# Sums of shared parts in two GpSimd operations instead of three, and masks made one step later

## The chip, the cores and the metric

The kernel runs on one core of a Trainium2 chip. The core's engines work side by side, each through its own list of instructions in order: TensorE (PE in the profile, with its weight loads as PEld), VectorE (DVE), ScalarE (ACT), GpSimd (POOL) and SyncE (SP), which here issues nearly all the DMAs. Engines wait for each other by semaphores. The metric is device time in microseconds; the kernel before takes 681.6 us (median of four runs, 679.55 to 683.3).

## The reference

Two blocks follow each other. The first is a delta-rule recurrence over 768 steps for 4 batches and 8 heads of width 48. In each step, with k normalised to length one:

```python
y[t]  = q[t] @ state
v_old = k[t] @ state
state = state + beta[t] * outer(k[t], v[t] - v_old)
```

The second takes the 4 x 768 outputs as 3072 tokens of width 384 and applies two dense layers with a hard swish between:

```python
h = x @ w_in                       # 384 -> 2048
g = h * clip(h + 3, 0, 6) / 6
out = g @ w_out                    # 2048 -> 384
```

## The kernel before

**The recurrence in chunks.** Time is cut into 24 chunks of 32 steps. The 4 batches times 32 steps fill the 128 partitions. For each chunk t a generator `prep(t)` makes what does not depend on the state, in steps: (1) GpSimd normalises the keys (`kb`, L502) and, where `whole` is set, makes the masks of the chunk at once (`mask(t)`, two multiplications at L478: beta times a fixed mask, for the even and the odd heads, into the tile `mb`); (2) TensorE transposes the keys (L518), ScalarE copies them to `KQ` (L526); (3) the same for the queries; (4) TensorE forms all products of keys with keys and queries (`sc`, L539); (5) VectorE multiplies them by the masks (L550, into `L` and `LB`), and GpSimd scales the keys by beta (`bkb`, L490). L550 is the only reader of `mb`, and `mb` has one buffer from chunk 9 on, so the masks of t wait until L550 of t-1 has read its own.

`chain(t)` then carries the state through the chunk (products with the state `ks` L798, `R` on VectorE at L892 and L898, `pz` and `py` L819, the update `su` L927, the output `y` L811 and L854, its transposition `yt` L864), and `inverse(g)` solves small triangular systems for four chunks at a time, element by element on VectorE (L751 and L756, alternating).

**The dense layers in blocks.** Two chunks make a block of 256 tokens. From block 5 on, `up_by_eleven` does the first layer by a scheme of Strassen's kind: for each of 8 products j it forms 2 x 2 tiles of 128 x 128 outputs out of 11 matmuls instead of 12. `begin(j)` issues the first four, which are parts shared by several outputs. ScalarE copies them from PSUM into the four quarters of a tile `g` (`gt`, L1069), and GpSimd adds them up there by `plus_minus` (L1020). `end(j)` issues the other seven matmuls on top of the same PSUM tile, and VectorE adds the sums from `gt` to PSUM tiles 3, 1 and 2 (L1085, L1086). ScalarE copies tile 0 (L1092), which lets the PSUM tile go, and makes the clipped factor (L1096); VectorE multiplies (L1099). PSUM tiles of this pool (`ph`, `pt`, `pz`, `py`, `yt`, `po`) come from one ring of four. `down_by_seven` does the second layer likewise with 7 products instead of 8 (L1211), sums on VectorE (L1197), and the sums of its outputs on GpSimd, on VectorE in the last block (both L1221). `weight_sums` makes sums of weights on GpSimd (also L1020, on 128x256) before the first such block.

**What sets the order.** The order of instructions on every engine is fixed when the program is built. A list written out by hand (`ORDER`) covers the first part. A loop over chunks follows, which cuts each chunk into 15 units and issues in each unit at most one step of `prep`, of `chain`, of the inverse and of the dense layers. `take(now)` in a unit's plan is one step of the chunk's `prep`. `plus_minus`, the masks, `kb`, `bkb`, the squares of keys (L401) and the output's sums share GpSimd's list, so what is issued first there is in front. Masks of chunks before the ninth are placed by `ORDER` and not by `prep`.

Of the kernel before, what the change touches and what calls it, by code (L numbers as in the profile page):

```python
# [15 lines left out]
ALU = mybir.AluOpType  # L16
# [30 lines left out]
def kernel(  # L47
# [21 lines left out]
    nc = tc.nc  # L69
# [3 lines left out]
    P = B * C  # L73
# [23 lines left out]
    def rows(b):  # L97
        return slice(C * b, C * b + C)
# [4 lines left out]
    def group(t):  # L103
        return (0, t) if t < G0 else ((t - G0) // GS + 1, (t - G0) % GS)
# [34 lines left out]
    def needs(*what):  # L139
        assert past.issuperset(what), (what, set(what) - past)  # L140
# [3 lines left out]
    def ring(tag, n, key):  # L144

        alive = [x for x in rings.get(tag, ()) if ("read", x) not in past]
        needs(*(("read", x) for x in alive[: max(len(alive) + 1 - n, 0)]))
        rings[tag] = alive + [key]
# [56 lines left out]
    for j, value in enumerate((1.0, -1.0)):  # L205
        m = mask2[:, j, :]
        for b in range(B):
            nc.gpsimd.memset(mask2[rows(b), j, :], value)
            nc.gpsimd.affine_select(
                out=mask2[rows(b), j, :], in_=mask2[rows(b), j, :], pattern=[[1, C]],  # L210
# [78 lines left out]
    def pad(t):  # L289
        return [f"pad{t}"] if t < NBKB else []  # L290
# [176 lines left out]
    def mask(t):  # L467
        early = t < LS + LE
        if t > 1 or not early:
            needs(("L", t - (2 if early else 1)))  # L470
        if early and t % 2 == 0:
            mb = mb_spare.rearrange("p (e a j w) -> p e a j w", e=2, j=2, w=C)
        else:
            mb = work.tile([P, 2, NP, 2, C], FP32, name="mb", bufs=1)
        mbs[t] = mb
        needs("beta")
        for e in range(2):
            nc.gpsimd.tensor_tensor(  # L478
                out=mb[:, e],
                in0=beta_tok[:, t, e:H:2].unsqueeze(2).unsqueeze(3).to_broadcast([P, NP, 2, C]),  # L480
                in1=mask2[:].unsqueeze(1).to_broadcast([P, NP, 2, C]),
                op=ALU.mult,
            )
        yield
# [12 lines left out]
    def prep(t, whole=True):  # L497

        g, i = group(t)
        kb, qb = kbufs[t % NKB], qbufs[t % NQB]  # L500
        needs(*([("bkb", t - NKB)] if t >= NKB else []), *(pad(t) if t < NKB and t else []))
        nc.gpsimd.tensor_tensor(  # L502
            out=kb[:, :, 0:D], in0=kfs[g][:, i],
            in1=invs.pop(t).unsqueeze(2).to_broadcast([P, H, D]), op=ALU.mult,
        )
        past.add(("kb", t))
        if whole:
            drain(mask(t))
        yield

        for j, src in enumerate((kb, qb)):
            if j == 1:
                needs(("q", t))
                past.add(("qT", t))
            ring("pm", NPM, ("pt", t, j))
            pt = psM.tile([128, NP, P], FP32, name="pt", tag="pm")
            for p in range(NP):
                nc.tensor.transpose(  # L518
                    pt[:, p, :], src[:, 2 * p : 2 * p + 2].rearrange("p e w -> p (e w)"), ident[:]
                )  # L520
            yield 1
            if j == 0:
                ring("KQ", NKQ, ("KQ", t))
                KQ = work.tile([128, NP * B // 2, 4, C], FP32, name="KQ", bufs=NKQ)
            read(("pt", t, j))
            nc.scalar.activation(  # L526
                out=KQ[:, :, 0:4:3, :] if j == 0 else KQ[:, :, 1:3, :],
                in_=pt[:].rearrange("q p (x y c) -> q (p x) y c", y=2, c=C), func=ACTF.Copy,
            )
            yield  # L530
        ring("pc", NPC, ("sc", t))
        sc = psC.tile([P, 2, 512], FP32, name="sc", tag="pc")
        scv = sc[:, :, 0 : NP * 2 * C].rearrange("p e (a j w) -> p e a j w", a=NP, j=2)
        for p in range(NP):
            for b in range(B):
                for e in range(2):
                    r = slice(DP * e, DP * e + DP)
                    kq = KQ[r, p * B // 2 + b // 2]
                    nc.tensor.matmul(  # L539
                        scv[rows(b), e, p],  # L540
                        lhsT=kq[:, 3 if b % 2 else 0, :],
                        rhs=kq[:, 3:1:-1, :] if b % 2 else kq[:, 0:2, :],
                        start=True, stop=True,
                    )
        yield
        needs(*([("BZ", t - NLB)] if t >= NLB else []))
        LB = work.tile([P, H, C], FP32, name="LB", bufs=NLB)
        mb = mbs.pop(t)
        for j, out in enumerate((lowers(t), LB)):
            nc.vector.tensor_tensor(  # L550
                out=out.rearrange("p (e a) w -> p e a w", e=2), in0=scv[:, :, :, j, :],
                in1=mb[:, :, :, j, :], op=ALU.mult,
            )
        past.add(("L", t))
        KQs[t], LBs[t] = KQ, LB
        read(("sc", t), *([("KQ", 0)] if t == 0 else []))
        if whole:
            drain(scaled(t))
        yield
# [459 lines left out]
    def plus_minus(out, a, b, op):  # L1019
        nc.gpsimd.tensor_tensor(out=out, in0=a, in1=b, op=op)  # L1020
# [28 lines left out]
    def up_by_eleven(blk):  # L1049
        needs(("sums", blk))  # L1050
        B11, T3x, B21, B22, B31, B32 = x_tiles(blk)
        phs, ready = {}, {}

        def mm(ph, n, w, x, start=False, stop=False):
            nc.tensor.matmul(  # L1055
                ph[:, n], lhsT=w, rhs=x, start=start, stop=stop, skip_group_check=True
            )

        def begin(j):
            key = ("ph", blk, "by", j)  # L1060
            ring("pm", NPM, key)
            ph = phs[j] = psM.tile([128, 4, P], FP32, name="ph", tag="pm")
            mm(ph, 0, W11[:, j], B11, start=True)
            mm(ph, 1, S1[:, j], T1x)
            mm(ph, 2, W21[:, j], T3x)
            mm(ph, 3, S2[:, j], T2x)
            gs[blk, j] = mlp.tile([128, 2, TB], FP32, name="g", bufs=NFC // 2)
            gt = gs[blk, j][:].rearrange("p i (t c) -> p (i t) c", c=P)
            nc.scalar.activation(out=gt, in_=ph[:], func=ACTF.Copy)  # L1069
            plus_minus(gt[:, 1], gt[:, 1], gt[:, 2], ALU.add)  # L1070
            plus_minus(gt[:, 2], gt[:, 0], gt[:, 1], ALU.add)
            plus_minus(gt[:, 0], gt[:, 0], gt[:, 3], ALU.add)

        def end(j):
            ph = phs.pop(j)
            mm(ph, 0, W12[:, j], B21)
            mm(ph, 1, S4[:, j], B22)
            mm(ph, 2, W22[:, j], T4x)
            mm(ph, 0, W13[:, j], B31)
            mm(ph, 1, W13[:, j], B32)  # L1080
            mm(ph, 2, W23[:, j], B31)
            mm(ph, 3, W23[:, j], B32, stop=True)
            g = gs[blk, j][:].rearrange("p i c -> p (i c)")
            gt = gs[blk, j][:].rearrange("p i (t c) -> p (i t) c", c=P)
            nc.vector.tensor_tensor(out=gt[:, 3], in0=ph[:, 3], in1=gt[:, 2], op=ALU.add)  # L1085
            nc.vector.tensor_tensor(  # L1086
                out=gt[:, 1:3], in0=ph[:, 1:3],
                in1=gt[:, 0].unsqueeze(1).to_broadcast([128, 2, P]), op=ALU.add,
            )

            def first():
                nc.scalar.activation(out=gt[:, 0], in_=ph[:, 0], func=ACTF.Copy)  # L1092
                read(("ph", blk, "by", j))
                ro = mlp.tile([128, CB, DM], FP32, name="o", bufs=1)
                r = ro[:].rearrange("p c m -> p (c m)")[:, 0 : 2 * TB]
                nc.scalar.activation(out=r, in_=g, func=ACTF.Relu, bias=half, scale=1.0 / 6.0)  # L1096

                def rest():
                    nc.vector.scalar_tensor_tensor(  # L1099
                        out=g, in0=r, scalar=1.0, in1=g, op0=ALU.min, op1=ALU.mult  # L1100
                    )

                ready[j] = rest

            ready[j] = first
            if j == NPR - 1:
                past.add(("up", blk))

        def go(j):
            if j in ready:  # L1110
                ready.pop(j)()

        begin(0)
        yield
        begin(1)
        yield
        for j in range(NPR):
            end(j)
            go(j - 1)
            if j + 2 < NPR:  # L1120
                yield
                begin(j + 2)
                go(j)
                yield
            else:
                go(j)
                if j == NPR - 1:
                    go(j)
                yield
# [197 lines left out]
    def drain(gen):  # L1327
        for _ in gen:
            pass
# [197 lines left out]
```

## Time and profile before

| | before |
|---|---|
| median of four runs | 681.6 us (679.55 to 683.3) |
| the profiled execution, its own time | 680.79 us |
| its span in the profile | 679.1 us |
| mean granted TensorE clock | 0.985 |
| PE, PEld busy | 640.5 us (94%), 581.1 us (86%) |
| DVE, ACT, POOL busy | 499.4 us (74%), 271.9 us (40%), 221.0 us (33%) |
| sums of shared parts (L1020 on g), 168 times | 79.8 us, mean 477 ns |
| masks (L478 into mb), 38 times | 26.9 us, mean 728 ns |
| additions to PSUM (L1085, L1086), 56 times each | 16.0 us, mean 285 ns; 23.8 us, mean 425 ns |

The profile is of one execution. Busy times of an engine are unions of its instructions' durations, and times in the text are counted from the start of the span. A group of instructions is named by line, engine and what it writes and reads (out<-in). Behind it stand how often it ran, its busy time and the mean of one, and the time that the engine stood idle just before, with what ended most of it. A row of a wait reads: who waited, for whom, total, how often, longest. A row of a timeline reads: start, duration, engine, line, operation, shapes, how many were merged. The blocks that use `up_by_eleven` start at about 342, 393, 445, 496, 544, 591 and 637 us. Each is followed by its `down_by_seven`.

### The profile page before, as it was taken

To read this page: it belongs to the slowest core of one execution; us is meant where nothing else is said; L and a number is where in the kernel's file an instruction comes from. 1 tells how busy PE (TensorE), PEld (TensorE's weight loads), DVE (VectorE), ACT (ScalarE), POOL (GpSimd) and SP (SyncE) were. 2 spreads that over 40 slices of the span, in tenths; PEclk is the share of its full clock that TensorE was granted. 3 is DMA by queue.
4 is the path that set the end of the run, shared out by engine and by line. 5 is a ranking of instruction groups with operands and counts; after the bars stand their busy time and mean duration, and the time that the engine had idled before them with its cause. 6 is when DMAs were issued, how large, how long until landed. Compare 5 with 4: busy or idle time off the path is not lost.

```text
span 679.1 us, 26940 instructions
## 1 busy us (share of the span) xinstructions
PE 640.5 (94%) x11768; PEld 581.1 (86%) x11768; DVE 499.4 (74%) x1226; ACT 271.9 (40%) x532; POOL 221.0 (33%) x376
## 2 busy tenths in 40 slices
PE   2668989999999999999999999999999999999997
PEld 2557877776688988988999999999999999999997
DVE  5888876888546689747888957998747998557264
ACT  5995777422242232232244244244234143143250
POOL 6240232102421131236165255065043151442340
PEclk9978889999999999999999999999999999999999
DMA  7994335502041030032030030020020020010000
GB/s 195 252 204 128 91 76 147 85 2 47 15 84 26 3 70 4 2 71 37 3 69 6 2 73 2 3 61 3 2 49 3 2 48 2 14 26 3 26 1 23
DMA packets 88501, 33.29 MB, mean 49 GB/s; under 512 B 80160, under 2 KB 83232, under 8 KB 88384
## 3 DMA queue, kind: packets, MB, share of 16 engines
q1 hardware_dynamic: 88128, 31.29, 20.8%
q8 instruction: 92, 1.51, 0.9%
q10 hardware_dynamic: 256, 0.30, 0.2%
q14 instruction: 25, 0.20, 0.1%
HBM read 26.84 MB, written 4.72 MB: 46 GB/s over the span
## 4 chain that ended last, share of the span: by engine, by line
PE 81%; DVE 7%; DMA 3%; ACT 2%; issue 2%; SPq 2%; POOL 1%; DVEq 0%; ACTq 0%; POOLq 0%
PE po L1211 26%; PE ph L1055 16%; PE ph L983 14%; PE po L1146 6%; PE pz L819 3%; PE ks L798 3%; PE py L819 3%; PE su L927 3%; PE pt L518 2%; PE sc L539 2%; SPq L1135 1%; ACT spare L348 1%; PE yt L864 1%; DMA out_dram<-o 1%; DMA kf<-in_k_dram 1%
## 5 line engine op out<-in xcount | busy, mean ns | idle before, releaser
L1055 PE MATMUL ph<-xT,w_in 128*128 128x128 f32 x784 | 122.9, 278 | 0.7 <-ACT KQ L526 0.7
L983 PE MATMUL ph<-xT,w_in 128*128 128x256 f32 (+1 forms) x576 | 116.2, 353 | 2.0 <-DVE g L994 1.5
L1211 PE MATMUL po<-w_out,g 128*128 128x192 f32 x640 | 110.6, 326 | 0.0
L983 PEld LDWEIGHTS ph<-xT,w_in 128*128 128x128 f32 x576 | 95.0, 194 | 14.3 <-DVE g L994 2.3
L1055 PEld LDWEIGHTS ph<-xT,w_in 128*128 128x128 f32 x784 | 103.9, 192 | 2.1 <-ACT KQ L526 0.9
L1020 POOL TENSOR_TENSOR g<-g 128x128 f32<-128x128 f32 x168 | 79.8, 477 | 76.5 <-ACT g L1069 67.3
L1211 PEld LDWEIGHTS po<-w_out,g 128*128 128x128 f32 x640 | 104.1, 190 | 0.2
L1211 PE MATMUL po<-spare,g 128*128 128x192 f32 x480 | 86.7, 332 | 0.0
L1211 PEld LDWEIGHTS po<-spare,g 128*128 128x128 f32 x480 | 77.2, 190 | 1.8
L1221 POOL TENSOR_TENSOR o<-o,u 128x192 f32<-128x192 f32 x18 | 18.6, 1033 | 167.3 <-ACT o L1218 93.5
L991 ACT ACTIVATE g<-ph,halves 128x256 f32<-128x256 f32 (+1 forms) x96 | 41.1, 436 | 79.1 <-PE ph L983 79.1
L1197 DVE TENSOR_TENSOR g<-g 128x256 f32<-128x256 f32 x160 | 62.8, 442 | 3.5 <-PE po L1211 3.1
L1069 ACT ACTIVATE g<-ph 128x512 f32<-128x512 f32 x56 | 33.4, 596 | 79.6 <-PE ph L1055 76.1
L756 DVE TENSOR_TENSOR A<-A,pr 128x30 f32<-128x30 f32 (+9 forms) x150 | 59.3, 395 | 3.6
L751 DVE TENSOR_TENSOR pr<-A 128x30 f32<-128x30 f32 (+9 forms) x150 | 56.1, 374 | 3.4
L348 ACT ACTIVATE spare<-spare,places 128x768 uint16<-128x768 uint16 (+1 forms) x56 | 52.4, 940 | 2.2 <-DMA spare<-in_moe_w_in_dram 1.3
L994 DVE SCALAR_TENSOR_TENSOR g<-g,ph 128x256 f32<-128x256 f32 (+1 forms) x96 | 35.0, 370 | 24.3 <-ACT g L991 24.1
L1099 DVE SCALAR_TENSOR_TENSOR g<-o,g 128x512 f32<-128x512 f32 x56 | 42.1, 751 | 8.1 <-ACT o L1096 8.1
L1096 ACT ACTIVATE o<-g,halves 128x512 f32<-128x512 f32 x56 | 40.4, 722 | 15.6 <-DVE g L1099 8.6
L1146 PE MATMUL po<-w_out,g 128*128 128x384 f32 x128 | 45.6, 493 | 0.0
L1218 ACT ACTIVATE o<-po 128x192 f32<-128x192 f32 x40 | 13.2, 330 | 80.6 <-PE po L1211 76.3
L478 POOL TENSOR_TENSOR mb<-beta_tok,mask 128x256 f32<-128x256 f32 x38 | 26.9, 728 | 56.2 <-DVE LB L550 56.2
(141 smaller groups left out, 991.2 us busy)
## 6 DMA issues: line engine op xcount, KB each, us to landing
kf<-in_k_dram SPq DMA_DIRECT2D x96, 48.0 KB, 3.0
qb<-in_q_dram SPq DMA_DIRECT2D x96, 48.0 KB, 3.1
vf<-in_v_dram SPq DMA_DIRECT2D x96, 48.0 KB, 2.2
out_dram<-o SPq DMA_DIRECT2D x92, 48.0 KB, 1.6
spare<-in_moe_w_in_dram SPq DMA_DIRECT2D x4, 768.0 KB, 6.7
w_out<-in_moe_w_in_dram SPq DMA_DIRECT2D x4, 768.0 KB, 6.3
w_out<-in_moe_w_out_dram SPq DMA_DIRECT2D x4, 768.0 KB, 6.1
spare<-in_moe_w_out_dram SPq DMA_DIRECT2D x4, 768.0 KB, 4.6
```

The source lines that it names most:

```text
L348: nc.scalar.activation(out=z, in_=z if n else d.bitcast(I16)[:, :, :, 3], func=func, bias=places[:, n : n + 1], scale=scale,)
L751: nc.vector.tensor_tensor(out=pv, in0=A[:, j + 1 :, j].unsqueeze(2).to_broadcast([n, w, j]), in1=A[:, j, 0:j].unsqueeze(1).to_broadcast([n ...
L756: nc.vector.tensor_tensor(out=A[:, j + 1 :, 0:j], in0=A[:, j + 1 :, 0:j], in1=pv, op=ALU.subtract)
L819: nc.tensor.matmul(ps[rows(place(b)), D * h : D * h + D], lhsT=m(h)[rows(b)], rhs=z[rows(b), D * at(h) : D * at(h) + D], start=True, stop= ...
L983: nc.tensor.matmul(ph[:, cols], lhsT=w_in[:, s, f * 128 : (f + 1) * 128], rhs=xT[:, s, cols], start=(s == 0), stop=(s == NKT - 1),)
L991: nc.scalar.activation(out=g, in_=ph, func=ACTF.Relu, bias=half, scale=1.0 / 6.0)
L1020: nc.gpsimd.tensor_tensor(out=out, in0=a, in1=b, op=op)
L1055: nc.tensor.matmul(ph[:, n], lhsT=w, rhs=x, start=start, stop=stop, skip_group_check=True)
L1099: nc.vector.scalar_tensor_tensor(out=g, in0=r, scalar=1.0, in1=g, op0=ALU.min, op1=ALU.mult)
L1146: nc.tensor.matmul(pos[c][:], lhsT=gs[blk, f // 2][:, f % 2, c * P : (c + 1) * P], rhs=w_out[:, f, :], start=(f == 0), stop=(f == NFC - 1),)
L1197: nc.vector.tensor_tensor(out=A(f, *out), in0=A(f, *a), in1=A(f, *b), op=op)
L1211: nc.tensor.matmul(ps[n][:], lhsT=A(f - f % 2, *a)[:, f % 2], rhs=b[:, f], start=(f == 0), stop=(f == HF - 1),)
```

## The change

It has two parts. In `begin`, with p0 to p3 for the four copied quarters of `gt`, the three additions before leave p1+p2 in quarter 1, p0+p1+p2 in quarter 2 and p0+p3 in quarter 0. After, one addition over two quarters at once, taken in descending order, leaves p0+p3 in quarter 3 and p1+p2 in quarter 2, and a second one leaves p0+p1+p2 in quarter 0. `end` is changed to match: the addition over two tiles, which now takes quarter 3, comes first, and the single one, which takes quarter 0, second. In `prep`, the masks are made in the step in which the transposed keys are copied, and no longer in the step in which the keys are normalised.

```diff
@@ prep @@
         past.add(("kb", t))
-        if whole:
-            drain(mask(t))
         yield
...
                 in_=pt[:].rearrange("q p (x y c) -> q (p x) y c", y=2, c=C), func=ACTF.Copy,
             )
+            if whole and j == 0:
+                drain(mask(t))
             yield
@@ up_by_eleven, begin @@
             nc.scalar.activation(out=gt, in_=ph[:], func=ACTF.Copy)
-            plus_minus(gt[:, 1], gt[:, 1], gt[:, 2], ALU.add)
-            plus_minus(gt[:, 2], gt[:, 0], gt[:, 1], ALU.add)
-            plus_minus(gt[:, 0], gt[:, 0], gt[:, 3], ALU.add)
+            plus_minus(gt[:, 3:1:-1], gt[:, 0:2], gt[:, 3:1:-1], ALU.add)
+            plus_minus(gt[:, 0], gt[:, 0], gt[:, 2], ALU.add)
@@ up_by_eleven, end @@
-            nc.vector.tensor_tensor(out=gt[:, 3], in0=ph[:, 3], in1=gt[:, 2], op=ALU.add)
             nc.vector.tensor_tensor(
                 out=gt[:, 1:3], in0=ph[:, 1:3],
-                in1=gt[:, 0].unsqueeze(1).to_broadcast([128, 2, P]), op=ALU.add,
+                in1=gt[:, 3].unsqueeze(1).to_broadcast([128, 2, P]), op=ALU.add,
             )
+            nc.vector.tensor_tensor(out=gt[:, 3], in0=ph[:, 3], in1=gt[:, 0], op=ALU.add)
```

## The prediction

> **What bounds the kernel now.** I read first the page's busy shares, then the chain of work that ended last, then a table of the seven stages in which the edited code runs (stretches of the span, with the busy time of each engine), then who TensorE (PE) waited for after 336 us, and at last single rows of GpSimd (POOL) and VectorE (DVE).
>
> ```profile
> PE 640.5 (94%) x11768; PEld 581.1 (86%) x11768; DVE 499.4 (74%) x1226; ACT 271.9 (40%) x532; POOL 221.0 (33%) x376
> PE 81%; DVE 7%; DMA 3%; ACT 2%; issue 2%; SPq 2%; POOL 1%; DVEq 0%; ACTq 0%; POOLq 0%
> ```
>
> POOL is busy a third of the span, and 1% of the last chain is its. The stages with the edited sums (the first three columns are the stretch, its length and PE's busy time; then weight loads, DVE, ACT, POOL):
>
> ```profile
> 342.00:369.00 27.00, 26.18 (x509) 25.31 (x509) 23.38 (x54) 13.03 (x26) 16.39 (x31) 1.00 0.23 46
> 393.50:420.00 26.50, 26.50 (x513) 25.81 (x512) 16.73 (x36) 13.25 (x27) 15.67 (x31) 1.00 0.25 48
> 445.00:472.00 27.00, 25.98 (x504) 24.86 (x504) 24.29 (x56) 12.88 (x27) 16.51 (x30) 1.00 0.19 39
> 496.00:522.00 26.00, 24.85 (x440) 24.21 (x439) 15.22 (x36) 12.45 (x25) 10.94 (x25) 1.00 0.16 33
> 544.50:570.00 25.50, 24.67 (x438) 24.04 (x437) 22.99 (x59) 12.68 (x25) 11.74 (x24) 1.00 0.16 34
> 592.00:616.50 24.50, 24.50 (x437) 23.90 (x437) 12.94 (x32) 12.57 (x25) 10.87 (x24) 1.00 0.12 27
> 637.50:660.00 22.50, 22.50 (x194) 22.50 (x194) 10.97 (x25) 12.27 (x25) 11.54 (x25) 1.00 0.07 19
> ```
>
> PE fills three of the seven to the last hundredth. In the others it lacks 0.8, 1.0, 1.2 and 0.8 us. Who it waited for from 336 us to the end:
>
> ```profile
> PE pz L819 <- DVE R L898: 2.2, 3, 1.1
> PE ph L1055 <- ACT KQ L526: 0.7, 1, 0.7
> PE py L819 <- issue: 0.6, 1, 0.6
> PE pz L819 <- ACT o L1218: 0.4, 1, 0.4
> PE yt L864 <- DVE y L854: 0.4, 1, 0.4
> ```
>
> POOL is not among them. All five together are 4.3 us of 343; the rows that name DVE are 2.6. DVE is said to wait for the edited sums:
>
> ```profile
> DVE g L1085 <- POOL g L1020: 14.4, 6, 2.8
> ```
>
> These six waits belong to the first two products of the stages at 496, 592 and 637 us. In the last of these, L1085 starts at 640.93, 643.38, 645.81 and 648.27, 2.45 us apart, the pace of PE's eleven matmuls, and only the first two are put down to POOL. The first product's three sums ended at 640.5 (two sets of three from 638.99, 2.99 us long), 0.45 us before L1085 began. So DVE waited for PE's last matmul there too, and the name POOL misleads. Of the gaps of PE, the one at 506.5 us (in the stage at 496) goes back through R (L898), which stands on DVE behind the product g<-o,g (L1099), to the wait of ACT L1096 for the output's DMA: the sums have no part in it.
>
> **The change, part by part.**
>
> *Two sums for three.* L1020 runs 168 times on 128x128 tiles, 79.8 us busy, 477 ns mean, three per product, 56 products. The trace has no GpSimd operation over two tiles in descending order. Nearest by form are the sums of weights on the same line, 128x256 from two tiles, 727 ns (median of the four rows 725 to 728). Bounds: the mask rows of the same size take 617 (median); the slowest plain add, o<-o,u at L1221, has a mean of 1033 ns on 192 elements, scaled to 256 some 1380. I take 727 since it is the same operation and size. A product then costs 727 + 477 = 1204 against 3 x 477 = 1431: 0.23 us less, 56 x 0.23 = 12.7 us of POOL time (bounds 19 less and 24 more). On the path: nothing, as POOL is not what PE waits for. The cover is the product itself: eleven matmuls of 224 ns (the last 176 rows, 88 loads and 88 matmuls, took 19.71 us), 2.46 us a product, in which POOL now works 1.52 us for a product and would work about 1.25.
>
> *The two DVE additions change places.* L1085 takes 0.29 us, L1086 0.42, and both still come before the ACT copy L1092. Before, the first waited for two POOL sums by what it read, and the second for the third; by the new order the first writes both middle tiles, one of which the second POOL sum reads, so it waits for both POOL sums, and the second adds nothing to wait for. Sum 0.71 us as before. I cost it at nothing: DVE comes to L1085 at PE's pace, with the sums 0.45 us ready. If a sum were late after all, the next cover is the ring of four PSUM tiles; past that room, each 0.1 us by which DVE is late costs PE 0.1 us a product, 5.6 us over 56. The ring's room: in the last stage the first product's tile is let go by L1092 at 642.48 and wanted by the fifth product at 645.5 (637.2 + 4 products' beginnings of 0.9 and 3 ends of 1.57, PE never idle), 3.0 us later.
>
> *The masks one step later.* By the order of the two programs on each engine, only five of the masks pass anything on POOL. Apart from the swapped additions no other engine's order changes; DMA queues and SP hold the same issues in the same order. The three in the edited stages:
>
> ```profile
> 345.38 0.98 POOL L502 TENSOR_TENSOR kb<-kf,inv 128x384 f32<-128x384 f32 x1
> 346.33 1.34 POOL L478 TENSOR_TENSOR mb<-beta_tok,mask 128x256 f32<-128x256 f32 x2
> 347.63 3.36 POOL L1020 TENSOR_TENSOR g<-g 128x128 f32<-128x128 f32 x6
> 351.62 1.80 POOL L1020 TENSOR_TENSOR g<-g 128x128 f32<-128x128 f32 x3 [0.63 <-ACT g L1069]
> 355.95 0.42 DVE L550 TENSOR_TENSOR L<-sc,mb 128x256 f32<-128x256 f32 x1
> ```
>
> The six sums that stood behind the mask now stand ahead of it. The first set can start at 346.4; the second needs the ACT copy that ends at 348.2, so it ends near 349.5; the mask then runs to about 350.8, and L550, its only reader, asks at 355.95: 5.1 us of room. Behind the mask stand the sums that wait for ACT until 351.55 anyway. At 396 and 447 the same count gives ends at 401.9 (copy ended 399.55, sums to 400.7) and 453.0, against readers at 406.22 and 458.45: 4.3 and 5.4 us. Cost nothing; the cover is that room. The third set's copies there end at 402.88 and 454.44, later than the masks. The fourth move lets six sums of weights (727 ns) pass a mask that waits for LB until 304.55:
>
> ```profile
> 293.62 0.83 POOL L502 TENSOR_TENSOR kb<-kf,inv 128x384 f32<-128x384 f32 x1
> 304.69 1.19 POOL L478 TENSOR_TENSOR mb<-beta_tok,mask 128x256 f32<-128x256 f32 x2 [10.24 <-DVE LB L550]
> ```
>
> POOL sits idle there for 10.24 us; six sums fit into it, and the later sums end some 4 us sooner. Their reader is the stage at 342 and the last of them still waits for the addition at 328, so: nothing. The fifth move, near 175 us, puts one square (0.82) ahead of a mask that ends at 176.8 and is read at 184.66: nothing.
>
> *What is left is who disturbs whom on DVE.* The product L1099, a DVE operation with both inputs in SBUF, takes 0.68 us in most rows, and long ones lie where POOL is at work:
>
> ```profile
> 357.82 1.24 DVE L1099 SCALAR_TENSOR_TENSOR g<-o,g 128x512 f32<-128x512 f32 x1
> 368.15 1.22 DVE L1099 SCALAR_TENSOR_TENSOR g<-o,g 128x512 f32<-128x512 f32 x1
> ```
>
> Of its 56 rows, the 44 that hardly overlap POOL have a median of 682 ns; the 12 that do average 1001. So less POOL time is less DVE time where DVE has no idle. In the stage at 342, DVE works without a gap from 342.7 to R's second half (L898, 351.96), for which PE waits 0.25 us at 352.7. POOL drops about 3 x 0.23 = 0.7 us before it; DVE operations in it run at about 0.55 against 0.41 (the L751 and L756 rows on 234 to 240 elements), a third longer, so DVE gains 0.2 us, and so does PE. The same at 466.7, where PE waits 0.4 us for y (L854) behind a full DVE: 0.1 us. At 554 the wait goes back to the output's DMA as at 506: nothing. Sum: 0.3 us gained. Ends for this effect: a gain of the whole 2.6 us that PE waits for DVE. Against it, a longer POOL operation can hold a DVE operation longer: the 12 disturbed L1099 rows each by the added 727 - 477 = 0.25 us, 3.0 us lost if all of it lay ahead of PE.
>
> Here a page speaks against the change: the Trainium skill, "SBUF — State Buffer", section "Who interferes with whom", says that a DVE operation with two SBUF inputs and a GpSimd operation that reads SBUF shut each other out for a whole instruction, whichever began first. By it the longest hold grows with the POOL operation, and the sum would be 3 us slower instead of 0.3 us faster. The rows above (1.24 against 0.68) fit a hold of about one POOL operation, but do not tell how often one strikes.
>
> **Sum.** The profiled execution took 680.8 us (span 679.1 and 1.7 around it); less 0.3 gives 680.5. It lies 0.8 under the median of 681.6, so against the median I say 681.3. The four runs spread from 679.55 to 683.3, about 0.5%, which is what a measurement of this kernel can tell from no change (3.4 us).
>
> **The rivals.**
> *Faster:* all that PE waits for DVE goes. For: DVE is at 23.4, 24.3 and 23.0 us in the three crowded stages. Against: at 506 and 554 a DMA sets the wait. It gives 681.6 - 2.6 = 679.0. To pass 0.5% the two ACT rows, 1.1 us, would have to go too (677.9).
> *Slower, by holds on DVE:* one longer POOL operation a product holds the crowded DVE, R and y come late, PE waits at L819 and L864. It decides from the point where DVE loses more than the 2.5 to 3.6 us that it has idle in a crowded stage, or where a hold falls just ahead of L898. Price up to 3.0 us: 684.6.
> *Slower, by the descending order:* if the wide sum is no 727 ns but over 1.85 us, a product needs more than its 2.46 us on POOL, and lateness grows from product to product until the ring's 3 us are used up. At 3.0 us it would be 1.15 x 8 - 3 = 6 us a stage, 7 stages, over 720 us. Against: no add in the trace comes near that.
> *The change does nothing that counts:* POOL's time falls and all else stays: 681.6.
>
> **Chances.** Forecast with the case that nothing counts 0.78 (680.5 to 682, and the spread of the runs); faster rival 0.08, half of it past 0.5% by scatter; holds on DVE 0.11, a third past 0.5%; descending order 0.03. So faster 0.04, slower 0.07, same 0.89. The range takes both ends of the DVE effect: 679.0 to 684.4.
>
> **What would show it.** Right: L1020 with 56 wide rows near 0.73 us and 56 at 0.46 to 0.48, together near 67 us; L1085 still 2.45 us apart in the last stage, whomever its waits are put down to; no L550 row that waits for a mask; POOL's sums of weights from 294 us; PE's waits still these five. Wrong: a wide row over 1.4 us, L1099's mean above 751 ns, a PE wait for L898 or L854 longer than now, or a new PE wait ahead of L1055. It would be wrong altogether if a change to POOL's order moved PE somewhere before 336 us, where DVE and ACT set the pace.

## The result and the profile after

The changed kernel is slower: a median of 682.9 us against 680.6 for the kernel before on the same chips, a ratio of 1.0028 with a 95% interval of 1.0018 to 1.0037. The two medians lie 2.3 us apart; the ratio is some 1.9 us, and that is the figure used below. The forecast was 0.3 us faster.

The profiled execution after has a span of 679.4 us. From its page, the busy shares, the edited sums and the two rows of the eliminations:

```profile
PE 640.5 (94%) x11768; PEld 581.1 (86%) x11768; DVE 501.4 (74%) x1226; ACT 272.4 (40%) x532; POOL 210.3 (31%) x320
...
L1020 POOL TENSOR_TENSOR g<-g 128x256 f32<-128x256 f32 x112 | 69.2, 619 | 85.7 <-ACT g L1069 81.3
...
L756 DVE TENSOR_TENSOR A<-A,pr 128x30 f32<-128x30 f32 (+9 forms) x150 | 61.5, 410 | 3.6
L751 DVE TENSOR_TENSOR pr<-A 128x30 f32<-128x30 f32 (+9 forms) x150 | 56.3, 376 | 3.4
```

GpSimd (POOL) does 10.7 us less, where 12.7 were forecast (the row of L1020 holds 56 sums of 256 elements and 56 of 128). VectorE (DVE) does 2.0 us more, with the same number of instructions. The row that grew is the eliminations' L756: 61.5 us against 59.3 before. It was not touched by the change.

The stages in which DVE is full of eliminations, in the table of stages of the kernel after (stretch, length, then PE, weight loads, DVE, ACT, POOL):

```profile
342.00:369.00 27.00, 25.97 (x506) 24.81 (x505) 23.66 (x55) 12.67 (x26) 14.62 (x22) 1.00 0.23 46
445.00:472.00 27.00, 25.18 (x499) 24.04 (x498) 24.43 (x55) 13.06 (x26) 14.34 (x21) 1.00 0.19 39
496.00:522.00 26.00, 26.00 (x448) 25.40 (x447) 15.95 (x38) 12.67 (x26) 10.44 (x18) 1.00 0.15 33
544.50:570.00 25.50, 24.26 (x435) 23.61 (x434) 23.20 (x58) 12.52 (x25) 10.31 (x16) 1.00 0.15 34
```

In the three full ones PE lacks 1.0, 1.8 and 1.2 us, where it lacked 0.8, 1.0 and 0.8. At 496 it lacks nothing, where it lacked 1.2. Who PE waited for after 336 us, in the kernel after:

```profile
PE pz L819 <- DVE R L898: 3.0, 4, 1.3
PE yt L864 <- DVE y L854: 1.1, 2, 0.5
PE ph L1055 <- ACT KQ L524: 0.2, 1, 0.2
```

The two waits for DVE were 2.2 and 0.4 us. Of the 2.2, 1.1 stood at 506 us, behind the output's DMA, and is gone.

Where DVE loses its time can be read row by row. DVE's rows in the kernel before, as the stage at 445 begins, and the three sums that POOL ran beside them:

```profile
444.94 0.40 DVE L756 TENSOR_TENSOR A<-A,pr 128x240 f32<-128x240 f32 x1
445.38 0.41 DVE L751 TENSOR_TENSOR pr<-A 128x240 f32<-128x240 f32 x1
445.82 0.55 DVE L756 TENSOR_TENSOR A<-A,pr 128x240 f32<-128x240 f32 x1
446.39 0.55 DVE L751 TENSOR_TENSOR pr<-A 128x238 f32<-128x238 f32 x1
446.98 0.55 DVE L756 TENSOR_TENSOR A<-A,pr 128x238 f32<-128x238 f32 x1
```

```profile
445.58 1.68 POOL L1020 TENSOR_TENSOR g<-g 128x128 f32<-128x128 f32 x3 [0.95 <-ACT g L1069]
```

The same work in the kernel after, and POOL's rows beside it:

```profile
445.23 0.40 DVE L756 TENSOR_TENSOR A<-A,pr 128x240 f32<-128x240 f32 x1
445.67 0.41 DVE L751 TENSOR_TENSOR pr<-A 128x240 f32<-128x240 f32 x1
446.11 0.82 DVE L756 TENSOR_TENSOR A<-A,pr 128x240 f32<-128x240 f32 x1
446.96 0.55 DVE L751 TENSOR_TENSOR pr<-A 128x238 f32<-128x238 f32 x1
447.54 0.92 DVE L756 TENSOR_TENSOR A<-A,pr 128x238 f32<-128x238 f32 x1
```

```profile
445.87 1.38 POOL L1020 TENSOR_TENSOR g<-g 128x256 f32<-128x256 f32 x2 [0.94 <-ACT g L1069]
447.21 0.99 POOL L502 TENSOR_TENSOR kb<-kf,inv 128x384 f32<-128x384 f32 x1
448.16 1.46 POOL L1020 TENSOR_TENSOR g<-g 128x256 f32<-128x256 f32 x2
```

An elimination of 0.41 us takes 0.55 beside a sum of 128 elements, 0.82 beside one of 256, and 0.92 beside the keys' 384. Before, DVE met three short sums and lost 0.14 us at each. After, it loses 0.41 at the wide one and 0.14 at the narrow one. So it reaches R (L898) later, and PE's first matmul of `pz` in this stage starts at 455.30 before and at 456.25 after, of which 0.3 us is the later start of the stage itself:

```profile
455.30 0.88 PE L819 MATMUL pz<-R,X 32*32 32x48 f32 x64
```

```profile
456.25 0.88 PE L819 MATMUL pz<-R,X 32*32 32x48 f32 x64 [1.27 <-DVE R L898]
```

All eliminations after 338 us give the same picture, if they are sorted by what POOL was doing when each of them began. In the table, the extra time of a row is its duration less that of the shortest row of its line and shape in the kernel before. One row in each kernel, which began beside a sum of outputs (o<-o,u), stands below the table.

| the elimination began | kernel | rows | mean extra, ns | longest extra, ns |
|---|---|---|---|---|
| with no POOL operation beside it | before | 92 | 9 | 63 |
| before a sum of 128 elements that overlaps it | before | 8 | 7 | 12 |
| before a sum of 256 elements that overlaps it | after | 14 | 6 | 12 |
| while a sum of 128 ran | before | 34 | 155 | 262 |
| while a sum of 128 ran | after | 11 | 148 | 155 |
| while a sum of 256 ran | after | 15 | 441 | 535 |
| while a mask of 256 ran | before | 8 | 355 | 432 |
| while scaled keys of 384 ran | before | 2 | 515 | 515 |

So it counts which of the two began first. An elimination that began before the sum lost nothing. One that began while a POOL operation ran lost what was left of that operation, less some 135 ns (118 to 142 ns in 84 of 85 rows of the two kernels, beside sums, masks and keys; the other row began 40 ns before a sum's end and lost nothing). The sums take 455 ns on 128 elements and 731 on 256 (medians), so the longer operation has more left when an elimination meets it. The row left out, in each kernel, began with 0.8 us of the sum of outputs left and lost nothing. That sum took 1.24 us before and 0.98 after, where most rows of its kind take about 0.6.

### The profile page after: what moved, and what is told of

Same layout as the page of the kernel before. It is cut to its first block, busy times and chain, and to the rows that moved or that the text cites. A ratio compares the mean times of both kernels' runs of the same rounds, so it can differ in the third digit from the quotient of the medians.

```text
span 679.4 us, 26872 instructions
## 1 busy us (share of the span) xinstructions
PE 640.5 (94%) x11768; PEld 581.1 (86%) x11768; DVE 501.4 (74%) x1226; ACT 272.4 (40%) x532; POOL 210.3 (31%) x320
## 5 line engine op out<-in xcount | busy, mean ns | idle before, releaser
L1020 POOL TENSOR_TENSOR g<-g 128x256 f32<-128x256 f32 x112 | 69.2, 619 | 85.7 <-ACT g L1069 81.3
L991 ACT ACTIVATE g<-ph,halves 128x256 f32<-128x256 f32 (+1 forms) x96 | 41.5, 437 | 79.8 <-PE ph L983 79.7
L756 DVE TENSOR_TENSOR A<-A,pr 128x30 f32<-128x30 f32 (+9 forms) x150 | 61.5, 410 | 3.6
L751 DVE TENSOR_TENSOR pr<-A 128x30 f32<-128x30 f32 (+9 forms) x150 | 56.3, 376 | 3.4
L1084 DVE TENSOR_TENSOR g<-ph,g 128x256 f32<-128x256 f32 x56 | 23.4, 418 | 38.1 <-PE ph L1055 27.1
L1098 DVE SCALAR_TENSOR_TENSOR g<-o,g 128x512 f32<-128x512 f32 x56 | 40.6, 726 | 7.4 <-ACT o L1095 7.4
```

The lines of the kernel that those rows point to most:

```text
L751: nc.vector.tensor_tensor(out=pv, in0=A[:, j + 1 :, j].unsqueeze(2).to_broadcast([n, w, j]), in1=A[:, j, 0:j].unsqueeze(1).to_broadcast([n ...
L756: nc.vector.tensor_tensor(out=A[:, j + 1 :, 0:j], in0=A[:, j + 1 :, 0:j], in1=pv, op=ALU.subtract)
L991: nc.scalar.activation(out=g, in_=ph, func=ACTF.Relu, bias=half, scale=1.0 / 6.0)
L1098: nc.vector.scalar_tensor_tensor(out=g, in0=r, scalar=1.0, in1=g, op0=ALU.min, op1=ALU.mult)
```

## The experiments

Each ratio is to the kernel before on the same chip. Two sizes are used beside it. "Stage" is the time in one profiled execution from a block's first matmul of the first layer to the next block's; the three full ones are those at 342, 445 and 544 us. "Extra" is the sum of the extra times of the 150 eliminations after the first of these stages begins.

| kernel | ratio (95% interval) | full stages, us | extra, us |
|---|---|---|---|
| before | 1 | 51.35, 51.75, 47.68 | 11.0 |
| before, again | 1.0002 (0.9981 to 1.0023) | 51.13, 51.82, 47.68 | 11.1 |
| after | 1.0028 (1.0018 to 1.0037) | 51.69, 52.47, 48.10 | 14.3 |
| sums only | 1.0030 (1.0013 to 1.0047) | 52.11, 52.59, 48.07 | 14.0 |
| masks only | 1.0008 (0.9988 to 1.0028) | 51.08, 51.64, 47.68 | 10.8 |
| three sums, additions swapped | 0.9986 (0.9968 to 1.0005) | 50.94, 51.53, 47.68 | 11.1 |
| wide, ascending | 1.0011 (0.9987 to 1.0035) | 52.05, 52.32, 48.10 | 14.0 |
| wide where DVE is full | 1.0017 (0.9993 to 1.0040) | 52.34, 52.30, 48.10 | 14.3 |
| wide where DVE is idle | 0.9984 (0.9959 to 1.0008) | 51.26, 51.68, 47.68 | 10.9 |
| shorter GpSimd operations | 0.9961 (0.9937 to 0.9986) | 50.65, 50.62, 47.68 | 8.2 |
| the same, again | 0.9953 (0.9931 to 0.9974) | 50.65, 50.48, 47.68 | 8.1 |
| the same, masks late | 0.9956 (0.9934 to 0.9977) | 50.14, 50.54, 47.68 | 8.4 |
| the same, wide sums | 0.9972 (0.9950 to 0.9993) | 51.07, 51.58, 48.09 | 12.0 |
| six short sums | 0.9932 (0.9906 to 0.9958) | 50.67, 50.71, 46.79 | 5.4 |

**The parts alone.** The first kernel has the sums and the swapped additions of the change and the masks of before:

```diff
-            plus_minus(gt[:, 1], gt[:, 1], gt[:, 2], ALU.add)
-            plus_minus(gt[:, 2], gt[:, 0], gt[:, 1], ALU.add)
-            plus_minus(gt[:, 0], gt[:, 0], gt[:, 3], ALU.add)
+            plus_minus(gt[:, 3:1:-1], gt[:, 0:2], gt[:, 3:1:-1], ALU.add)
+            plus_minus(gt[:, 0], gt[:, 0], gt[:, 2], ALU.add)
...
+                in1=gt[:, 3].unsqueeze(1).to_broadcast([128, 2, P]), op=ALU.add,
             )
+            nc.vector.tensor_tensor(out=gt[:, 3], in0=ph[:, 3], in1=gt[:, 0], op=ALU.add)
```

> The two-for-three sums and the swapped additions, with the masks made where the kernel before makes them. Theory LENGTH (a GpSimd sum over 256 elements holds a VectorE operation with two SBUF inputs longer than one over 128): this part alone carries the loss, ratio to before 1.002 to 1.004, and the elimination rows L751 and L756 after 336 us sum to over 62.5 us against 60.6 of before. Rival PLACE (the moved masks collide with the work ahead of R): ratio 0.999 to 1.001 and the sum within 0.7 us of 60.6. Rival ORDER (the 256-wide addition first costs VectorE): loss as with LENGTH, but the elimination rows stay at 60.6.

It carries the whole loss: 1.0030, eliminations after 336 us 63.9 us. Its group of L756 and what PE waited for:

```profile
L756 DVE TENSOR_TENSOR A<-A,pr 128x30 f32<-128x30 f32 (+9 forms) x150 | 62.2, 415 | 3.6
```

```profile
PE pz L819 <- DVE R L898: 3.6, 4, 1.2
PE yt L864 <- DVE y L854: 1.1, 2, 0.5
```

LENGTH is what it should be, and PLACE is out for this part. The second has the masks alone:

```diff
-        if whole:
-            drain(mask(t))
         yield
...
+            if whole and j == 0:
+                drain(mask(t))
             yield
```

> Only the masks are made one step later; three sums and the order of additions as before. LENGTH: ratio 0.999 to 1.001, elimination rows after 336 us within 0.7 us of 60.6. PLACE: ratio 1.002 to 1.004, and the gap of TensorE ahead of pz (L819, waiting for R L898) in the stages at 342 and 445 grows by 0.5 us or more. ORDER: 1.000.

The ratio is 1.0008 with an interval on both sides of one, the eliminations sum to 60.8 us, and the stages are no longer than before. Nothing of the loss is shown to come from the masks. In this kernel PE waited for R only at 554 us:

```profile
PE pz L819 <- DVE R L898: 0.8, 1, 0.8
PE yt L864 <- DVE y L854: 0.7, 2, 0.4
```

The third, shown against the first, keeps the changed kernel's quarters and its order of additions, and makes the wide sum in two again:

```diff
-            plus_minus(gt[:, 3:1:-1], gt[:, 0:2], gt[:, 3:1:-1], ALU.add)
+            plus_minus(gt[:, 3], gt[:, 0], gt[:, 3], ALU.add)
+            plus_minus(gt[:, 2], gt[:, 1], gt[:, 2], ALU.add)
             plus_minus(gt[:, 0], gt[:, 0], gt[:, 2], ALU.add)
```

> Three sums over 128 elements again, but into the quarters of the changed kernel and with its order of the two additions on VectorE; masks as before. LENGTH and PLACE: ratio 0.999 to 1.001, elimination rows within 0.7 us of 60.6. ORDER: ratio 1.002 to 1.004.

Its ratio of 0.9986, eliminations of 61.1 us and L756 of 59.4 us speak against ORDER: the loss went with the wide operation alone. The first and the third kernel ran side by side and differ in nothing but the wide sum. Their medians are 681.7 and 679.3 us, 2.4 us apart; in their profiles the full stages differ by 2.6 us. This pair shows the cost of the wide sum better than a comparison with the kernel before, for a reason given under what stays open.

```profile
L756 DVE TENSOR_TENSOR A<-A,pr 128x30 f32<-128x30 f32 (+9 forms) x150 | 59.4, 396 | 3.6
```

The kernel before, once more, beside these:

> The kernel before once more, under another name. All theories: ratio 0.999 to 1.001. If it comes out at 1.002 or more, the loss of 0.28% is not told apart from loading a program again (rival NOTHING).

It came out at 1.0002. It also shows how much of a stage can be trusted: the stages at 342 and 445 differ by 0.2 and 0.1 us between the two executions.

**Is it the descending order?** The wide sum in ascending order, with the masks at their old place:

```diff
-            plus_minus(gt[:, 3:1:-1], gt[:, 0:2], gt[:, 3:1:-1], ALU.add)
+            plus_minus(gt[:, 2:4], gt[:, 0:2], gt[:, 2:4], ALU.add)
```

> As the sums alone with masks at their old place, but the wide sum takes its two pairs in ascending order (quarter 0 with 2 into 2, quarter 1 with 3 into 3). The sums are then other ones than the scheme needs, so the outputs differ from the reference's; the work is the same in size. Theory LENGTH (what counts is that a GpSimd operation reads 256 elements in one go): as with the sums alone, stage at 342 near 52.0 us and stage at 445 near 52.5, elimination rows after 336 us 63 to 65 us, ratio 1.002 to 1.004. Rival DESCENDING (the reversed order of the pairs makes the hold): stages 51.1 and 51.7, elimination rows near 61, ratio 1.000.

The ratio, 1.0011 (0.9987 to 1.0035), does not decide. The stages and the extra do: 52.05, 52.32 and 48.10 us and 14.0 us, as with the descending sum.

```profile
L756 DVE TENSOR_TENSOR A<-A,pr 128x30 f32<-128x30 f32 (+9 forms) x150 | 62.3, 415 | 3.6
```

**Where is it lost?** The wide sum in three of the seven blocks; the converse has (6, 8, 10, 11) in the same line:

```diff
-            plus_minus(gt[:, 3:1:-1], gt[:, 0:2], gt[:, 3:1:-1], ALU.add)
+            if blk in (5, 7, 9):
+                plus_minus(gt[:, 3:1:-1], gt[:, 0:2], gt[:, 3:1:-1], ALU.add)
+            else:
+                plus_minus(gt[:, 3], gt[:, 0], gt[:, 3], ALU.add)
+                plus_minus(gt[:, 2], gt[:, 1], gt[:, 2], ALU.add)
             plus_minus(gt[:, 0], gt[:, 0], gt[:, 2], ALU.add)
```

> Wide sums only in blocks 5, 7 and 9 (stages at 342, 445 and 544 us, where VectorE is full with eliminations), three narrow ones in the other four. LENGTH with a full VectorE: the whole loss is here, ratio 1.002 to 1.004, stages 52.0, 52.5 and 48.1 us, elimination rows 63 to 65 us. Rival EVERYWHERE (each wide sum costs TensorE the same, 3/7 of the loss here): ratio 1.001.

> The converse: wide sums only in blocks 6, 8, 10 and 11, where VectorE has no eliminations beside them; three narrow ones in blocks 5, 7 and 9. LENGTH with a full VectorE: ratio 0.998 to 1.000 as with three sums and swapped additions, stages 51.0, 51.6 and 47.7 us. EVERYWHERE: ratio 1.002 (4/7 of the loss).

1.0017 and 0.9984: the intervals overlap a little, but the stages part cleanly. With 24 wide sums beside the eliminations the full stages are 52.34, 52.30 and 48.10; with 32 wide sums elsewhere they are 51.26, 51.68 and 47.68, as in the kernel before. The stages at 393, 496 and 591 do not lengthen there either (50.37, 46.78 and 45.97 us against 50.50, 46.79 and 45.97 with three sums). EVERYWHERE is out: a wide sum costs in the stages that DVE fills with eliminations. Whether it takes the eliminations or only a full DVE was not told apart. PE's waits for R and y in the first, and all that it waited for in the second:

```profile
PE pz L819 <- DVE R L898: 2.7, 3, 1.2
PE yt L864 <- DVE y L854: 1.1, 2, 0.5
```

```profile
PE pz L819 <- DVE R L898: 1.0, 2, 0.8
PE py L819 <- issue: 0.8, 2, 0.6
PE ph L1055 <- ACT KQ L526: 0.8, 1, 0.8
```

The second has no row for y.

**The other way round: shorter operations.** If length is the cause, cutting GpSimd's other operations must help, though it gives GpSimd more to do. With the three narrow sums, masks and keys of the chunks from the ninth on are cut in two:

```diff
+    def heads(t):
+        return [slice(0, H)] if t < LS + LE else [slice(0, H // 2), slice(H // 2, H)]
...
+        n = 2 if early else 1
         for e in range(2):
-            nc.gpsimd.tensor_tensor(
-                out=mb[:, e],
...
+            for a in range(0, NP, NP * n // 2):
+                w = NP * n // 2
+                nc.gpsimd.tensor_tensor(
+                    out=mb[:, e, a : a + w],
...
-        nc.gpsimd.tensor_tensor(
-            out=kb[:, :, 0:D], in0=kfs[g][:, i],
...
+        inv = invs.pop(t)
+        for r in heads(t):
+            nc.gpsimd.tensor_tensor(
+                out=kb[:, r, 0:D], in0=kfs[g][:, i, r],
...
```

> Three narrow sums and swapped additions, and the other GpSimd operations of the chunks from the ninth on cut in two as well: masks from 256 to 128 elements, normalised and scaled keys from 384 to 192. GpSimd gets some 4 x 0.19 us more work a chunk. LENGTH: each held elimination beside a mask or a key operation loses 0.13 to 0.26 us instead of 0.39 to 0.52, the extra time of the eliminations after 336 us falls from 11.4 to about 9 us, and the ratio is 0.995 to 0.999, under that of the three narrow sums alone. Rival AMOUNT (what counts is GpSimd's whole time): more time on GpSimd, ratio 1.000 to 1.002.

> The version with shorter GpSimd operations once more, on this chip. LENGTH: ratio 0.995 to 0.998, stages 50.65 and 50.62 us within 0.2. If the earlier 0.9961 was chance, 1.000.

0.9961, and 0.9953 the second time: faster than before, both intervals under one. After the first of the stages begins, POOL's busy time rises from 127.4 to 134.1 us, and DVE's falls from 244.1 to 239.1. AMOUNT is out. What the cut of masks and keys adds to the three narrow sums is smaller than these ratios say: the interval overlaps that of three sums (0.9986), and the full stages, 149.0 us together, are 1.2 us shorter than there. L756 and L751 stand at L768 and L763 in this kernel:

```profile
L768 DVE TENSOR_TENSOR A<-A,pr 128x30 f32<-128x30 f32 (+9 forms) x150 | 56.2, 374 | 3.6
L763 DVE TENSOR_TENSOR pr<-A 128x30 f32<-128x30 f32 (+9 forms) x150 | 54.4, 363 | 3.4
```

The same with the masks at their later place, and the same with the wide sums (the edits shown above, on top of this kernel):

> The version with shorter GpSimd operations, and the masks one step later as in the changed kernel. LENGTH: the place of the masks counts nothing, ratio 0.995 to 0.998, stages within 0.2 us of 50.65 and 50.62. PLACE: stages over 51 us.

> The version with shorter masks and keys, but with the wide sums of the changed kernel. LENGTH, if the holds add up: the stages at 342 and 445 lose again what they lost between three narrow sums and the wide one (1.1 us each, to some 51.8 and 51.7), 48.1 at 544, extra time of the eliminations near 11 us, ratio 0.998 to 1.000.

The masks' place again costs nothing; one stage is even 0.5 us shorter (50.14), which was not expected. The wide sum takes back 0.4, 1.0 and 0.4 us in the full stages and the ratio rises from 0.9953 to 0.9972 (intervals overlapping). That is less than the 1.1 us expected in each of two stages, and the extra of 12.0 us is a little more than expected: the holds add up only roughly. Why was not looked into.

Last, the sums in pieces of 64 elements, six operations a product:

```diff
-            plus_minus(gt[:, 3], gt[:, 0], gt[:, 3], ALU.add)
-            plus_minus(gt[:, 2], gt[:, 1], gt[:, 2], ALU.add)
-            plus_minus(gt[:, 0], gt[:, 0], gt[:, 2], ALU.add)
+            for o, a in ((3, 0), (2, 1)):
+                for r in (slice(0, P // 2), slice(P // 2, P)):
+                    plus_minus(gt[:, o, r], gt[:, a, r], gt[:, o, r], ALU.add)
+            for r in (slice(0, P // 2), slice(P // 2, P)):
+                plus_minus(gt[:, 0, r], gt[:, 0, r], gt[:, 2, r], ALU.add)
```

> As the version with shorter GpSimd operations, and each sum of 128 elements cut into two of 64: six a product. A product then takes GpSimd some 6 x 0.32 + gaps = 2.2 us against 2.46 us of matmuls. LENGTH: a held elimination loses at most 0.13 us, its extra time after 342 us falls from 8.2 to 5 to 7 us, and the stages at 342 and 445 stay at or under 50.6 us; ratio 0.994 to 0.998. Rival AMOUNT: the longer GpSimd time makes the sums late, stages over 51 us, ratio over 1.000.

0.9932 (0.9906 to 0.9958), 674.7 us against 679.8 for the kernel before on that chip: faster than both kernels of the change, and lower than was expected. The sums now take 103.4 us of POOL, against 79.8 before, and the extra of the eliminations is halved. The sums, L756 and L751 (L768 and L763 here), and all that PE still waited for:

```profile
L1032 POOL TENSOR_TENSOR g<-g 128x64 f32<-128x64 f32 x336 | 103.4, 343 | 46.9 <-ACT g L1081 46.8
...
L768 DVE TENSOR_TENSOR A<-A,pr 128x30 f32<-128x30 f32 (+9 forms) x150 | 54.5, 363 | 3.6
L763 DVE TENSOR_TENSOR pr<-A 128x30 f32<-128x30 f32 (+9 forms) x150 | 53.3, 355 | 3.4
```

```profile
PE ph L1067 <- ACT KQ L538: 0.4, 2, 0.3
```

Of the 31 eliminations that began while a 64-element sum ran, 27 lost at most 13 ns: nearly all had under 150 ns of the sum left. The stages at 342 and 445, 50.67 and 50.71, are no shorter than with sums of 128; what the shorter sums gained there is at 544, 46.79 against 47.68. The interval overlaps those of both runs with 128-element sums, so that this last step is worth anything in the median is likely and not shown.

**What stays open.** The full stages of the kernel after are 1.6 us longer than the mean of the two executions of before (152.3 against 150.7). But the stages at 393 and 496 are shorter, by 0.3 and 1.0 us, so that from the first of the seven stages to the last the kernel after took 295.4 us against 295.4 and 294.8: only 0.3 us more than the mean. The profiles thus show that the wide sum lengthens the full stages, and do not account for the 1.9 us between the medians of before and after. The time at which the first of these stages begins varies from 339.4 to 346.0 us between the profiled executions of these kernels, so what happens ahead of it can't be read from one profile.

The gain at 496 has nothing to do with the wide sum. In both profiles of the kernel before, and in no other, PE lost about a microsecond in that stage (48.0 and 47.6 us against 46.8): there SP took 5.1 and 4.5 us to issue eight output DMAs, and 3.6 in the kernels after, with masks only and with three sums. Why was not tried. If it is so in most executions of the kernel before, about 1 us of what the faster kernels won is this. That is open: the masks alone have the gain in their profile too, and are not faster in the median (1.0008).

## Why the prediction was wrong, point by point

*What bounds the kernel* held: PE fills the stages, and what can be won or lost is what it waits for DVE. *Two sums for three* held in size: a wide sum took 759 ns on average (the median is 731), the narrow one 479, and the whole row 69.2 us for the 67 forecast. That it costs nothing on the path was wrong. The cover was named for POOL's own lateness, and that cover held: no wait of PE is put down to a late sum. What was not covered was another engine. (The upper bound for the wide sum was read from a mean of 1033 ns for o<-o,u; twelve of these eighteen rows take about 0.6 us, and one of 4.3 us stands beside twelve operations of DVE in a row.)

*The two additions* held: 0.42 and 0.29 us, and no loss with the order alone (0.9986, one inside the interval). L1084 in the last stage starts at 641.13, 643.59, 646.24 and 648.47, PE's pace within 0.2 us, and the first is still put down to POOL. *The masks* held: the first ended at 351.3 for the 350.8 forecast and was read at 356.65, the sums of weights began at 294.6, and the part alone gave 1.0008 with one inside.

The step that failed is *what is left is who disturbs whom on DVE*: "POOL drops about 3 x 0.23 = 0.7 us before it; DVE operations in it run at about 0.55 against 0.41 (the L751 and L756 rows on 234 to 240 elements), a third longer, so DVE gains 0.2 us, and so does PE." It took the disturbance to go with POOL's total time. It goes with what is left of the single POOL operation that an elimination runs into: 0.41 us and more beside 256 elements, mostly 0.14 beside 128, and nothing for an elimination that began first. A product in which DVE met all the sums lost 3 x 0.14 us before and 0.41 + 0.14 after, though POOL worked less. In place of the 0.3 us gained, the wide sum cost 1.9 us against the kernel before and 2.4 us against three sums in the same quarters. The rows to see it were there: the masks of 256 elements and the keys of 384 already held eliminations for 355 and 515 ns on average in the kernel before, and the prediction used only the rows beside the sums for its slope.

One reading in the same passage was wrong as well. "At 554 the wait goes back to the output's DMA as at 506: nothing." At 506 it did, but at 554 DVE has no gap of over 0.1 us from 544.4 to 554.6. ScalarE's factor, which waited for the DMA, was done at 551.8, and DVE came to the product behind it only at 552.5:

```profile
552.53 0.94 DVE L1099 SCALAR_TENSOR_TENSOR g<-o,g 128x512 f32<-128x512 f32 x1
553.40 0.60 DVE L898 SCALAR_TENSOR_TENSOR R<-ks,parity,R 128x384 f32<-128x384 f32 x1
```

So this wait, too, is a full DVE. The stage is 47.68 us with sums of 128, 48.1 with wide ones and 46.79 with sums of 64.

The right case stood among the rivals as *slower, by holds on DVE*, with the right mechanism and the right waits, L819 and L864. Its price of up to 3.0 us holds the measured 1.9. It was worked out from the wrong rows, though: of the nine L1099 rows in the kernel before that began while POOL ran, seven stand beside the keys, whose length the change leaves as it is. The range's upper end, 684.4, also lies 0.2 us under this price (684.6), which it was meant to take in. Of its two conditions the second, "or where a hold falls just ahead of L898", is the one that was met: the prediction itself had read that DVE works without a gap from 342.7 to L898, and in the stages at 445 and 544 the first idle time after the eliminations begin is behind L898 too (455.9 and 554.8 us). A hold there counts at once. So the chance of 0.11 was too small by the prediction's own rows, and the forecast went for the case that nothing counts.

The page of the Trainium skill that was weighed, "SBUF — State Buffer", section "Who interferes with whom", had the sign right: its 3 us slower was nearer than 0.3 us faster. It says that the loser is shut out for the whole instruction. The rows here agree that the one that began first is not held, and have the elimination end sooner than that, by 118 to 142 ns: with 666 ns of a wide sum left it lost 535. Whether it is let in before the sum's end, or does a part of its own work meanwhile, the rows do not tell.

Of the signs, a longer wait of PE for L898 and L854 was named, and came. A longer L756 was not named. L1099's mean (L1098 after) was, and fell from 751 to 726 ns: the product still runs into the keys' operations, but later, with about 0.43 us of them left where 0.68 was left before. As a sign of what the sums do it was badly chosen.

## What to carry to other kernels

Where two engines shut each other out, cost a change by what can be left of the longest single operation and by what stands ahead of the waiting engine's next deadline, not by busy time: here fewer and longer GpSimd operations saved 10.7 us of GpSimd and lost 1.9 us, and more and shorter ones cost GpSimd 32 us (127.4 to 159.8 after the first stage begins) and won some 5, of which about 1 may be the stage at 496. An engine with two thirds of its time idle can afford the extra fixed cost if the engine it disturbs is full. Look for the rows of an untouched line that grow; they name the victim.

## What the runs showed of the hardware

An elimination on VectorE (both inputs in SBUF) that began while a GpSimd sum, mask or key operation ran lost what was left of that operation less 118 to 142 ns, in 84 of 85 rows of before and after; the other had 40 ns left and lost nothing. An elimination that began before an overlapping sum lost at most 12 ns (22 rows). GpSimd is held as well: a sum of outputs that takes about 0.6 us in most rows took 4.3 at 578 us in the kernel before, beside twelve VectorE operations (L1197, 4.1 us) in a row.

The sums' medians, 319, 455 and 731 ns on 64, 128 and 256 elements, give about 2.1 ns per element and some 180 ns that do not depend on their number. The reversed order of the two tiles cost GpSimd nothing: 731 ns, against 730 in ascending order.
